# Complex linear attention and two expert layers on one core: results kept in quarters of 32 rows, block ends multiplied in three levels

## The chip, the cores and the metric

The kernel runs on one core of a Trainium2 chip. The metric is the device time of one execution in microseconds (us). PE is TensorE, DVE is VectorE, ACT is ScalarE, POOL is GpSimd, and SP is the engine on whose queue nearly all transfers are issued.

## The reference

A recurrence with complex decay per channel over 768 steps for 4 batches of 8 heads of 48 channels, then a dense layer with `h * cos(h)`, then a layer of 8 experts of which each token takes one:

```
a_n = a * min(|a|, 0.999) / (|a| + 1e-6)
S   = a_n[t] * S + k[t] v[t]^T          # complex S, 48 x 48 a head
y[t] = q[t] . real(S)
x = y as [3072, 384];  h = x @ w_in;  g = h * cos(h);  x = g @ w_out
e = argmax(x @ w_gate);  out = gate * sigmoid * (relu(x @ w1[e]) @ w2[e])
```

## The kernel before, in words

The tokens are 24 chunks of 128, six to a batch, and two chunks make a unit, so there are 12 units. A unit passes three stages:

- **The scan** (`scan`): on DVE and ACT. `normal` makes the normalised decay out of `a_t` (with a reciprocal root on ACT, `root`), `core` multiplies the decays up in blocks of 8 by 8 (seven steps along the block, then the block ends, lines 305 to 317, then the ends into the blocks, lines 320 to 331), `inverse` makes the reciprocals (a second root on ACT, line 248), and `post` multiplies q and k. Twenty small DMAs (`out_`, lines 369 to 372) bring the result to the tiles `qkr`, by head. All elementwise products of `tt` have line 205 in the profile.
- **Attention** (`attn`): for each chunk PE turns k (line 423), multiplies scores `sc` (438), DVE masks them to `pt`, and PE multiplies the results: `pt` with v (457) and, from a batch's second chunk on, the carried state `tp` with q (462). Two heads stand in one column of `pv_t`, at rows 0 and 64, 48 rows each; ACT copies `pv_t` to `x` rounded (466) and DVE takes the rest (the low part of `x`). Heads 6 and 7 stand in a fourth column, and six DMAs a chunk (488, 489) bring them into the gaps of 16 rows that the other three columns leave. Then the state is updated (473) and its halves are exchanged by DMA (481, 482).
- **The dense layer**: in eight steps s a unit, `mm1` (509, 18 products of 128x256, three each of a high and a low part) waits for `x`; `act2` (517 to 519: square, sine, square) and `act3` (548) follow; `mm2` (564, 8 records) multiplies by w_out. The `h` tiles have two buffers, which `gated` (738 to 742, which multiplies w_out by the gates' weights, through ACT copies) also takes during unit 0. `weights` decodes the weights in the first units on DVE and ACT.

ACT holds one table of functions at a time: sine needs one and the reciprocal root another, and each change is an ACT_TABLE_LOAD. Routing scatters rows by expert to DRAM, and from some 700 us on the experts' products run (`second`). A scheduler of the tile framework orders the instructions of each engine by a simulation when the program is built; `behind` adds an order without a wait. Zero rows for the scatter (493, 495) are issued on SP behind the last of the six DMAs of units 1 and 2.

Of the kernel before, what the change touches and what calls it, by code (L numbers as in the profile page):

```python
# [79 lines left out]
def host_layout(x):  # L80

    f = np.float32
    d = {}
    pq, pa = order_q(), order_a()

    def scan(p, order):
        z = p.transpose(0, 1, 3, 2).reshape(B, DM, NCB, C)[:, channels()][..., order]
        z = z.reshape(B, 3, 128, UPB, UC, C).transpose(0, 3, 2, 4, 1, 5)
        return z.reshape(NU, 128, NCOL, C)

    d["a"] = np.ascontiguousarray(np.stack([scan(x["a_re"], pa), scan(x["a_im"], pa)], 2))
    d["qk"] = np.ascontiguousarray(np.stack([scan(x["q"], pq), scan(x["k"], pq)], 2))
    v = x["v"].transpose(0, 2, 1, 3).reshape(NCH, C, DM)[:, pq]
    d["v"] = np.ascontiguousarray(v)
    rows = np.zeros((3, 128), np.int64)
    for i in range(3):
        for p in range(128):
            h, e = 2 * i + p // 64, p % 64
            if e >= 48:
                h, e = 6 + p // 64, 16 * i + e - 48  # L100
# [24 lines left out]
    d["rk"] = rk  # L125
    d["xz"] = np.zeros((256, ROW), np.int32)
    d["xz"][:, NO] = NT
    d["xz"] = d["xz"].view(f)
    tok = np.zeros((NCH, 128), np.int32)
    for c in range(NCH):  # L130
        tok[c] = (c // NCB) * S + (c % NCB) * C + pq
    d["ids"] = np.ascontiguousarray(tok.T)
    return d


def build(tc, ap, out, force=False):
# [56 lines left out]
    nb = sp.tile([128, 2, 2 * NCOL, 8], F32, name="nb")  # L193
# [5 lines left out]
    fg = sp.tile([128, 3, 2, NCOL], F32, name="fg")  # L199
    qflat = qkt.rearrange("p a b c d -> p (a b c d)")  # L200

    pv_t = ps_v.tile([128, 4, 128], F32, name="pv_t")

    def tt(e, o, a, b, op):
        return e.tensor_tensor(out=o, in0=a, in1=b, op=op)  # L205
# [26 lines left out]

    rooted = set()

    def root(u):
        rooted.add(u)
        A.activation(out=a_t[:, 2], in_=nt[:, 1], func=AF.Abs_reciprocal_sqrt)

    def inverse(u, ua):

# [5 lines left out]
        mark["add", u] = tt(V, r, sq[:, 0], sq[:, 1], ADD)  # L246
        yield
        A.activation(out=y, in_=r, func=AF.Abs_reciprocal_sqrt)
        A.activation(out=q, in_=y, func=AF.Square)
        if ua is not None:  # L250
            root(ua)
        yield
        tt(V, r, r, q, MUL)
        yield
# [36 lines left out]
    def core(u):  # L291
# [10 lines left out]
            yield  # L302
        if u + 1 < NU:
            load_a(u + 1)
        V.tensor_scalar(out=nb[:, 0], in0=lb[:, 1, :, 7], scalar1=-1.0, scalar2=None, op0=MUL)
        V.tensor_copy(nb[:, 1], lb[:, 1, :, 7])
        V.tensor_copy(pb[:, :, :, 1], lb[:, :, :, 7, 0])
# [8 lines left out]
        V.tensor_scalar(out=nb[:, 0, :, 1:8], in0=pb[:, 1, :, 1:8], scalar1=-1.0, scalar2=None, op0=MUL)  # L316
        V.tensor_copy(nb[:, 1, :, 1:8], pb[:, 1, :, 1:8])
        yield
        k = 2 * n * 56
        t1, t2 = (qflat[:, k * i:k * (i + 1)].rearrange("p (r c j b) -> p r c j b", r=2, c=n, j=8) for i in range(2))  # L320
        bc = [128, n, 8, 7]
        for r in range(2):
            tt(V, t1[:, r], lb[:, r, :, :, 1:8], pb[:, 0, :, 1:8].unsqueeze(2).to_broadcast(bc), MUL)
            yield
            tt(V, t2[:, r], lb[:, 1 - r, :, :, 1:8], nb[:, r, :, 1:8].unsqueeze(2).to_broadcast(bc), MUL)
            yield
        sq = squares(u + 1) if u + 1 < NU else iter(())
        next(sq, None)
        la = l_t.rearrange("p r c (h j b) -> p (r c h) j b", h=2, j=8)[..., 1:8]
        tt(V, la, t1.rearrange("p r c j b -> p (r c) j b"), t2.rearrange("p r c j b -> p (r c) j b"), ADD)  # L330
        yield
        gates(u)
        yield
# [71 lines left out]
    x_t = {}  # L405
    st = {}

    def attn(u):
        x = xp.tile([128, 2, 4, UC * C], F32R, name="x")
        x_t[u] = x  # L410
        kn_t = {}
        vt = {}
        for cc in range(UC):
            vt[cc] = vp.tile([128, DM], F32, name="vt")
# [16 lines left out]
        for cc in range(UC):  # L431
            c = (u % UPB) * UC + cc
            pt = {}
            for g in range(2):
# [7 lines left out]
            tp = None  # L442
            if c > 0:
                s_, ss = st["s"], st["ss"]
                tp = at1.tile([96, H, D], F32, name="tp")
# [3 lines left out]
                tt(V, tp, s_, ss, ADD)  # L449
                yield  # L450
            for g in range(2):
                t = qkr[cc, g]
                for i in range(2):
                    pr = 2 * g + i
                    for hh in range(2):
                        h = 2 * pr + hh
                        PE.matmul(pv_t[64 * hh:64 * hh + 48, pr], lhsT=vt[cc][:, h * D:(h + 1) * D],
                                  rhs=pt[g][:, 2 * i + hh], start=True, stop=c == 0)
                    if c > 0:
                        for hh in range(2):  # L460
                            h = 2 * pr + hh
                            PE.matmul(pv_t[64 * hh:64 * hh + 48, pr], lhsT=tp[:, h],
                                      rhs=t[:, 2 * i + hh, 0, 0:C], start=False, stop=True)
            yield
            xs_ = x[:, :, :, cc * C:(cc + 1) * C]
            A.copy(xs_[:, 0], pv_t)  # L466
# [2 lines left out]
            if c < NCB - 1:  # L469
                m = ps_m.tile([128, 512], F32, name="m")  # L470
                mu = m[0:96, 0:DM].rearrange("p (h d) -> p h d", h=H)
                for h in range(H):
                    PE.matmul(mu[:, h], lhsT=kn_t[cc][:, h].rearrange("p r d -> p (r d)"), rhs=vt[cc][:, h * D:(h + 1) * D],  # L473
                              start=True, stop=True)
                s_ = at1.tile([96, H, D], F32, name="s_")
                ss = at1.tile([96, H, D], F32, name="ss")
                if c == 0:
                    A.copy(s_, mu)
                else:
                    tt(V, s_, mu, tp, ADD)  # L480
# [4 lines left out]
            xb = x.bitcast(F32)  # L485
            cs = slice(cc * C, (cc + 1) * C)
            for i in range(3):
                SY.dma_start(xb[48:64, :, i, cs], xb[16 * i:16 * i + 16, :, 3, cs])
                pad = SY.dma_start(xb[112:128, :, i, cs], xb[64 + 16 * i:64 + 16 * i + 16, :, 3, cs])
            if u in (1, 2) and cc == UC - 1:  # L490
                mark["pad"] = pad
                for a0 in range(NE * CAP // 2 * (u - 1), NE * CAP // 2 * u, 256):
                    behind(SY.dma_start(xs[a0:a0 + 256], ap["xz"]), "pad")
                if u == 1:
                    behind(SY.dma_start(xs0, ap["xz"]), "pad")
            yield


# [751 lines left out]
    if True:  # L1250
# [7 lines left out]
        V.memset(pv_t, 0.0)  # L1258
        V.tensor_copy(acc, smt[:, 1, 0])
        G.tensor_copy(top, smt[:, 3])  # L1260
        V.memset(eb, 0.0)
# [114 lines left out]
```

## Time and profile before

| | |
|---|---|
| median of 3 runs | 973.82 us (973.53 to 974.1) |
| the profiled execution, its own time | 972.88 us |
| its span, first to last instruction | 971.1 us |
| PE busy | 894.8 us (92%) |
| DVE busy | 664.3 us (68%) |
| ACT busy | 582.0 us (60%) |
| ACT_TABLE_LOAD by lines 518, 237, 248 | 20, 11 and 9, of 1283 ns each |
| DMAs of `x` into the gaps | 144, 16 KB each |

A row of a timeline begins with start and duration in us; xN is the number of records merged in it, and a bracket gives the idle time before it and what ended that. A product of 32-bit floats is two records on PE, one of the rounded type is one. A busy PE is not PE at its peak, so what a stretch costs is read from starts.

### The profile page before, as it was taken

What the parts mean: (1) busy time and instruction counts of PE and PEld (TensorE: products, weight loads), DVE (VectorE), ACT (ScalarE), POOL (GpSimd) and SP (SyncE); (2) the same over time, 40 slices, a digit from 0 to 9 for tenths busy, and PEclk for the clock granted to TensorE, in tenths of its full rate; (3) what the DMA queues carried; (4) which work ended last, traced back from release to release, by engine and by line L of the source; (5) the groups of instructions that cost most, each with busy time, mean ns of one, the idle gap of its engine ahead of it and who ended that gap; (6) DMA issues with size and microseconds to landing.
All of it is one profiled execution on the core that took longest, in us unless ns stands there. A gap on an engine that the chain in (4) does not pass through costs nothing.

```text
span 971.1 us, 16175 instructions
## 1 busy us (share of the span) xinstructions
PE 894.8 (92%) x5701; PEld 756.5 (78%) x5701; DVE 664.3 (68%) x1498; ACT 582.0 (60%) x1252; POOL 134.3 (14%) x246
## 2 busy tenths in 40 slices
PE   0566897999999999999999999999999999999997
PEld 0455685877777787777777778789899899999997
DVE  6989885887779786979698788445664553355521
ACT  6684866757574848585757665365773453355521
POOL 0010001002123002020312121101121110312111
PEclk9999999999999999999999999999999999999999
DMA  9813046345333223232333231440328532554100
GB/s 328 313 43 106 20 114 207 100 120 167 102 85 122 66 95 85 90 95 90 89 101 85 97 96 47 115 142 22 106 76 259 167 128 66 175 182 140 25 28 33
DMA packets 69789, 109.93 MB, mean 113 GB/s; under 512 B 14063, under 2 KB 51327, under 8 KB 69428
## 3 DMA queue, kind: packets, MB, share of 16 engines
q1 hardware_dynamic: 62724, 98.72, 32.9%
q0 software_dynamic: 6976, 10.10, 3.1%
q8 instruction: 47, 0.77, 0.3%
q14 instruction: 42, 0.34, 0.1%
HBM read 74.20 MB, written 21.86 MB: 99 GB/s over the span
## 4 chain that ended last, share of the span: by engine, by line
PE 50%; DVE 19%; ACT 11%; DMA 8%; issue 6%; SPq 4%; POOL 0%; DVEq 0%; another core or an unknown queue 0%; ACTq 0%; POOLq 0%
PE o L564 12%; PE h L952 10%; PE h L509 10%; PE p L976 6%; PE p L968 4%; DVE t L205 3%; DVE qkt L205 2%; DMA a_t<-in_a_dram 2%; PE sc L438 2%; DVE l_t L205 1%; DVE g L548 1%; DMA xs<-in_xz_dram 1%; DVE pt L205 1%; PE m L473 1%; DVE nt L205 1%
## 5 line engine op out<-in xcount | busy, mean ns | idle before, releaser
L509 PE MATMUL h<-x,wi 128*128 128x256 f32 x1728 | 247.7, 294 | 14.9 <-DMA x<-x 5.6
L564 PE MATMUL o<-wo,g 128*128 128x400 f32 x672 | 246.2, 506 | 0.0
L509 PEld LDWEIGHTS h<-x,wi 128*128 128x128 f32 x1728 | 218.9, 191 | 34.4 <-issue 8.7
L564 PEld LDWEIGHTS o<-wo,g 128*128 128x128 f32 x672 | 121.2, 192 | 72.2 <-issue 4.4
L952 PE MATMUL h<-xe,w1t 128*128 128x384 f32 (+6 forms) x576 | 118.7, 349 | 0.0
L956 DVE SCALAR_TENSOR_TENSOR hh<-h,hh 128x384 fp32r<-128x384 f32 (+6 forms) x64 | 37.2, 582 | 117.5 <-ACT hh L955 116.9
L952 PEld LDWEIGHTS h<-xe,w1t 128*128 128x128 f32 x576 | 101.8, 188 | 5.2
L517 ACT ACTIVATE g<-h 128x512 f32<-128x512 f32 x96 | 57.1, 594 | 79.6 <-PE h L509 75.7
L955 ACT ACTIVATE hh<-h 128x384 fp32r<-128x384 f32 (+6 forms) x64 | 32.8, 514 | 114.1 <-PE h L952 107.5
L548 DVE SCALAR_TENSOR_TENSOR g<-g,h 128x512 f32<-128x512 f32 x96 | 65.5, 682 | 43.5 <-ACT g L519 42.3
L572 POOL DMA_INDIRECT xs<-rows,si x46 | 55.7, 1211 | 172.0 <-ACT x L466 41.0
L976 PE MATMUL p<-w2t,hh 128*128 128x384 f32 (+1 forms) x384 | 76.7, 343 | 0.0
L976 PEld LDWEIGHTS p<-w2t,hh 128*128 128x128 f32 (+1 forms) x384 | 66.0, 186 | 1.5 <-DVE hh L956 0.3
L519 ACT ACTIVATE g<-g 128x512 f32<-128x512 f32 x96 | 60.8, 633 | 1.8
L438 PEld LDWEIGHTS sc<-qkr 96*128 96x128 f32 x384 | 51.5, 203 | 11.7 <-issue 3.5
L438 PE MATMUL sc<-qkr 96*128 96x128 f32 x384 | 57.0, 293 | 3.8 <-DMA qkr<-qkt 2.4
L518 ACT ACTIVATE g<-h 128x512 f32<-128x512 f32 x96 | 57.6, 600 | 1.8
L205 POOL TENSOR_TENSOR fg<-l_t,m 128x12 f32<-128x12 f32 x24 | 4.7, 215 | 373.5 <-DVE l_t L205 241.8
L572 POOL DMA_INDIRECT out_dram<-o,tok x28 | 34.6, 1234 | 149.6 <-issue 57.4
L968 PE MATMUL p<-hh,w2t 128*128 128x448 f32 (+2 forms) x216 | 47.6, 359 | 0.0
L205 DVE TENSOR_TENSOR t<-l_t,a_t 128x192 f32<-128x192 f32 x144 | 45.0, 352 | 1.4
L205 DVE TENSOR_TENSOR qkt<-l_t,qk_t 128x1536 f32<-128x1536 f32 (+1 forms) x26 | 41.2, 1630 | 0.3
(299 smaller groups left out, 1501.7 us busy)
## 6 DMA issues: line engine op xcount, KB each, us to landing
stg<-in_w_dram SPq DMA_DIRECT2D x32, 768.0 KB
qkr<-qkt SPq DMA_DIRECT2D x96, 146.2 KB
a_t<-in_a_dram SPq DMA_DIRECT2D x12, 768.0 KB
qk_t<-in_qk_dram SPq DMA_DIRECT2D x12, 768.0 KB
xs<-in_xz_dram SPq DMA_DIRECT2D x17, 401.0 KB
raw<-in_w_in_dram SPq DMA_DIRECT2D x7, 768.0 KB
raw<-in_w_out_dram SPq DMA_DIRECT2D x7, 768.0 KB
vt<-in_v_dram SPq DMA_DIRECT2D x24, 192.0 KB
```

The costliest lines, as they stand in the source:

```text
L205: return e.tensor_tensor(out=o, in0=a, in1=b, op=op)
L438: PE.matmul(sc[:, h], lhsT=t[:, h, 1, 0:C], rhs=t[:, h, 0, 0:C], start=True, stop=True)
L509: PE.matmul(h[:, i], lhsT=wis[s][:, wi, kk, i * 128:(i + 1) * 128], rhs=x_t[u][:, xi, kk], start=n == 0, stop=n == 8)
L517: A.activation(out=g, in_=h, func=AF.Square, accum_out=hck[:, u * NS + s:u * NS + s + 1])
L518: mark["sin"] = A.activation(out=g, in_=h, func=AF.Sin, scale=0.5)
L519: A.activation(out=g, in_=g, func=AF.Square, scale=float(np.sqrt(2.0)))
L548: V.scalar_tensor_tensor(out=g, in0=g, scalar=1.0, in1=hps.pop((u, s)), op0=SUB, op1=MUL)
L564: PE.matmul(o, lhsT=a[:, i, cs], rhs=w[:, i], start=s == 0 and n == 0 and i == 0, stop=s == NS - 1 and n == len(prods) - 1 and i == 1)
L572: sc = G.indirect_dma_start(in_offset=None, oob_is_err=False, **kw)
L952: PE.matmul(h, lhsT=w[:, wi, kk, f * 128:(f + 1) * 128], rhs=x[:, xi, kk], start=n == 0, stop=n == 8)
L968: PE.matmul(o2[e][d][:, 0:c], lhsT=w[:, wi, f, d * 128:(d + 1) * 128], rhs=hh[:, hi], start=f == 0 and n == 0, stop=f == KE - 1 and n == 2)
L976: mm = PE.matmul(o2[e][j][0:w_, 0:DM], lhsT=hh[:, hi, j * w_:(j + 1) * w_], rhs=w[:, wi, f], start=f == 0 and n == 0, stop=f == KE - 1 and ...
```

## The change

Each head's 48 results are split in 32 and 16. The first 32 of heads 0 to 3 fill the four quarters of column 0 of `pv_t`, those of heads 4 to 7 column 1, and the last 16 of two heads share a quarter of column 2. For the shared quarter v and the state get columns of zeros beside them (`vt` and `tp` become 4 pairs of 128), so that two products add up in one quarter. A product is 32 columns wide, and there are 32 instead of 16 in a chunk with a state, 16 instead of 8 in one without. `x` uses three of its four columns, the DMAs into gaps are gone, and the rows of w_in are laid out to match. The block ends are a product over distances 1, 2 and 4 in place of six steps in a row, and the negated copies `nb` are gone: sign is in SUB and ADD, and the last sum of `core` is two instructions. The root of unit u+1 is ordered behind the square of unit u's inverse.

```
-    pv_t = ps_v.tile([128, 4, 128], F32, name="pv_t")
+    pv_t = ps_v.tile([128, 3, 128], F32, name="pv_t")
+    tp = at1.tile([96, 4, 128], F32, name="tp")
+    tps = tp[:, :, 16:112]
...
-    def root(u):
+    def root(u, *after):
         rooted.add(u)
-        A.activation(out=a_t[:, 2], in_=nt[:, 1], func=AF.Abs_reciprocal_sqrt)
+        behind(A.activation(out=a_t[:, 2], in_=nt[:, 1], func=AF.Abs_reciprocal_sqrt), *after)
...
-        A.activation(out=q, in_=y, func=AF.Square)
+        mark["rs"] = A.activation(out=q, in_=y, func=AF.Square)
         if ua is not None:
-            root(ua)
+            root(ua, "rs")
...
-        for i in range(2, 8):
-            t1, t2 = t12[:, 0, :, 0:n], t12[:, 1, :, 0:n]
-            tt(V, t1, pb[:, :, :, i - 1], lb[:, 0:1, :, 7, i - 1].to_broadcast([128, 2, n]), MUL)
-            tt(V, t2, pb[:, ::-1, :, i - 1], nb[:, :, :, i - 1], MUL)
-            yield
-            tt(V, pb[:, :, :, i], t1, t2, ADD)
-            yield
+        for d, a, b in ((1, last[..., 1:7], last[..., 0:6]), (2, pb[..., 3:8], pb[..., 1:6]), (4, pb[..., 5:8], pb[..., 1:4])):
+            t1, t2 = (t12[:, i].rearrange("p r (c b) -> p r c b", b=8)[..., 0:7 - d] for i in range(2))
+            bc = [128, 2, n, 7 - d]
+            tt(V, t1, a, b[:, 0:1].to_broadcast(bc), MUL)
+            tt(V, t2, a, b[:, 1:2].to_broadcast(bc), MUL)
+            yield
+            tt(V, pb[:, 0, :, d + 1:8], t1[:, 0], t2[:, 1], SUB)
+            tt(V, pb[:, 1, :, d + 1:8], t1[:, 1], t2[:, 0], ADD)
+            yield
...
+            srcs = [(vt[cc], [pt[h // 4][:, h % 4] for h in range(H)])]
+            if c > 0:
+                srcs.append((tp, [qkr[cc, h // 4][:, h % 4, 0, 0:C] for h in range(H)]))
+            for kk in range(2):
+                for n, (a, r) in enumerate(srcs):
+                    for g in range(4):
+                        h = 4 * kk + g
+                        w = 32 + 32 * (h % 2)
+                        PE.matmul(pv_t[32 * g:32 * g + 32, kk], lhsT=a[:, h // 2, w:w + 32], rhs=r[h],
+                                  start=n == 0, stop=n == len(srcs) - 1)
+            for n, (a, r) in enumerate(srcs):
+                for odd in range(2):
+                    for g in range(4):
+                        PE.matmul(pv_t[32 * g:32 * g + 32, 2], lhsT=a[:, g, 96 * odd:96 * odd + 32], rhs=r[2 * g + odd],
+                                  start=n == 0 and odd == 0, stop=n == len(srcs) - 1 and odd == 1)
...
-            for i in range(3):
-                SY.dma_start(xb[48:64, :, i, cs], xb[16 * i:16 * i + 16, :, 3, cs])
-                pad = SY.dma_start(xb[112:128, :, i, cs], xb[64 + 16 * i:64 + 16 * i + 16, :, 3, cs])
```

The scheduler makes another order out of it. The rows below name lines of each kernel's own file; up to 3 lines lie between them. Three places follow.

ACT, unit 0, behind the second copy of `pv_t` to `x`. In the kernel before (466 is the copy; 227 and 228 square the decays of unit 2; 517 to 519 are `act2`):

```order
L466 CAST x<-pv_t 128x4x128
L227 ACTIVATE a_t<-a_t 128x768
L228 ACTIVATE nt<-a_t 128x768
L517 ACTIVATE g,hck<-h 128x512
L518 ACT_TABLE_LOAD
L518 ACTIVATE g<-h 128x512
L519 ACTIVATE g<-g 128x512
L517 ACTIVATE g,hck<-h 128x512
```

In the changed kernel (469 is the copy, 230 and 231 the squares, 514 to 516 `act2`):

```order
L469 CAST x<-pv_t 128x3x128
L514 ACTIVATE g,hck<-h 128x512
L515 ACT_TABLE_LOAD
L515 ACTIVATE g<-h 128x512
L516 ACTIVATE g<-g 128x512
L514 ACTIVATE g,hck<-h 128x512
L230 ACTIVATE a_t<-a_t 128x768
L231 ACTIVATE nt<-a_t 128x768
```

The first step's `act2` and the start of the second's now stand ahead of the squares.

PE, where unit 0's products meet unit 1's first scores. In the kernel before (423 turns k, 738 and 741 are `gated`, 438 the scores, 473 the state, 509 `mm1`):

```order
L423 MATMUL m<-ident,qkt 128x128 x3
L741 MATMUL h<-wg,raw 128x16 x3
L738 MATMUL h<-ident,raw 128x128 x3
L438 MATMUL sc<-qkr 128x128 x6
L473 MATMUL m<-vt,kn 96x48 x6
```

In the changed kernel (426 turns k, 735 and 738 are `gated`, 506 `mm1`, 476 the state, 441 the scores):

```order
L426 MATMUL m<-ident,qkt 128x128 x3
L735 MATMUL h<-ident,raw 128x128 x3
L506 MATMUL h<-x,wi 128x256 x18
L476 MATMUL m<-vt,kn 96x48 x8
L738 MATMUL h<-wg,raw 128x16 x3
L441 MATMUL sc<-qkr 128x128 x2
```

A whole step of `mm1` and one chunk's state now stand ahead of the scores.

ACT, the last two `gated` copies of unit 0 (742 with `rawr`; 244 to 249 are unit 2's `inverse`). In the kernel before:

```order
L742 COPY rawr<-h 128x16
L726 COPY wo<-rawr 128x16
L739 COPY rawr<-h 128x384
L244 ACTIVATE qkt<-l_t 128x1536
L517 ACTIVATE g,hck<-h 128x512
L518 ACT_TABLE_LOAD
L518 ACTIVATE g<-h 128x512
L248 ACT_TABLE_LOAD
L248 ACTIVATE qkt<-nt 128x768
L519 ACTIVATE g<-g 128x512
L742 COPY rawr<-h 128x16
```

In the changed kernel (739 with `rawr` is the same copy; 230 and 231 square the decays of unit 3):

```order
L739 COPY rawr<-h 128x16
L723 COPY wo<-rawr 128x16
L230 ACTIVATE a_t<-a_t 128x768
L231 ACTIVATE nt<-a_t 128x768
L736 COPY rawr<-h 128x384
L514 ACTIVATE g,hck<-h 128x512
L739 COPY rawr<-h 128x16
```

No table load stands between the two copies any more; the squares, which stood ahead of both before, stand between them.

## Rows read from the trace of the kernel before

**Rows 1.** The page's first line.
```profile
span 971.1 us, 16175 instructions
```

**Rows 2.** Busy time by stretch: length, then each engine's busy us, clock, DMA share.
```profile
0.00:180.00 180.00, 119.05 (x680) 97.64 (x681) 146.35 (x291) 122.81 (x267) 9.02 (x43) 0.97 0.46 155
180.00:610.00 430.00, 420.99 (x2854) 329.06 (x2854) 348.82 (x813) 282.97 (x600) 71.24 (x148) 1.00 0.33 97
610.00:971.00 361.00, 354.78 (x2169) 329.76 (x2167) 169.14 (x395) 176.20 (x386) 54.04 (x55) 1.00 0.35 112
```

**Rows 3.** Timeline of PE at the first unit's `mm1`.
```profile
93.22 0.77 PE L509 MATMUL h<-x,wi 128*128 128x256 f32 x2 [4.66 <-DMA x<-x]
104.68 0.51 PE L509 MATMUL h<-x,wi 128*128 128x256 f32 x2 [3.38 <-DVE g L548]
```

**Rows 4.** Timeline of ACT in the same stretch.
```profile
88.61 0.59 ACT L466 CAST x<-pv_t 128x512 fp32r<-128x512 f32 x1 [4.60 <-PE pv_t L462]
99.18 0.85 ACT L227 ACTIVATE a_t<-a_t 128x768 f32<-128x768 f32 x1 [9.99 <-DMA a_t<-in_a_dram]
```

**Rows 5.** Timeline of PE where units 0 and 1 meet.
```profile
132.66 1.68 PE L438 MATMUL sc<-qkr 96*128 96x128 f32 x12 [0.21 <-DMA qkr<-qkt]
...
151.00 2.39 PE L509 MATMUL h<-x,wi 128*128 128x256 f32 x18
...
156.20 0.63 PE L738 MATMUL h<-ident,rawr 128*128 128x128 f32 x3 [2.20 <-ACT raw L742]
156.87 4.65 PE L564 MATMUL o<-wo,g 128*128 128x400 f32 x8
...
170.25 2.03 PE L509 MATMUL h<-x,wi 128*128 128x256 f32 x10 [3.47 <-ACT rawr L742]
```

**Rows 6.** Timeline of ACT where units 0 and 1 meet.
```profile
121.85 0.24 ACT L358 COPY qkt<-fg 128x24 f32<-128x24 f32 x1
...
155.98 0.16 ACT L742 COPY raw<-h 128x16 f32<-128x16 f32 x1
...
167.48 1.28 ACT L248 ACT_TABLE_LOAD   x1
...
170.04 0.15 ACT L742 COPY rawr<-h 128x16 f32<-128x16 f32 x1
```

**Rows 7.** Timeline of DVE: first instruction of a block end, first behind it.
```profile
94.32 0.21 DVE L305 TENSOR_SCALAR nb<-l_t 128x96 f32<-128x96 f32 x1
...
98.53 0.85 DVE L205 TENSOR_TENSOR qkt<-l_t,pb 128x672 f32<-128x672 f32 x1
```

**Rows 8.** Groups of DVE by form: busy us, mean ns of one, idle before.
```profile
L205 DVE TENSOR_TENSOR t<-l_t,a_t 128x192 f32<-128x192 f32 x144 | 45.0, 352 | 1.4
...
L205 DVE TENSOR_TENSOR x<-pv_t,x 128x512 fp32r<-128x512 f32 x24 | 16.4, 682 | 1.5 <-ACT x L466 1.5
L205 DVE TENSOR_TENSOR pb<-t 128x24 f32<-128x24 f32 x72 | 14.6, 202 | 1.9
```

**Rows 9.** Timeline of PE, a lone run of scores and a run of results.
```profile
435.26 1.73 PE L438 MATMUL sc<-qkr 96*128 96x128 f32 x14
436.74 2.25 PE L509 MATMUL h<-x,wi 128*128 128x256 f32 x17
...
440.93 0.42 PE L457 MATMUL pv_t<-pt,vt 128*48 128x128 f32 x4
...
442.83 0.94 PE L564 MATMUL o<-wo,g 128*128 128x400 f32 x2
```

**Rows 10.** Timeline of PE, a run of results cut in two pieces.
```profile
146.95 0.43 PE L457 MATMUL pv_t<-pt,vt 128*48 128x128 f32 x4
147.31 0.94 PE L564 MATMUL o<-wo,g 128*128 128x400 f32 x2
```

**Rows 11.** Who waited for whom: us in total, times, longest.
```profile
DVE s__5808 L205 <- DMA x<-x: 5.4, 1, 5.4
```

**Rows 12.** Groups of ACT: busy us, mean ns of one, idle before.
```profile
L518 ACT ACT_TABLE_LOAD x20 | 25.7, 1283 | 0.3
```

More of the change, by code (lines that the diff above doesn't have):

```diff
@@ L92, in host_layout @@
     d["qk"] = np.ascontiguousarray(np.stack([scan(x["q"], pq), scan(x["k"], pq)], 2))
-    v = x["v"].transpose(0, 2, 1, 3).reshape(NCH, C, DM)[:, pq]
-    d["v"] = np.ascontiguousarray(v)
+    v = x["v"].transpose(0, 2, 1, 3).reshape(NCH, C, 4, 2, D)[:, pq]
+    d["v"] = np.zeros((NCH, C, 4, 128), f)
+    d["v"][..., 16:32], d["v"][..., 32:64] = v[..., 0, 32:], v[..., 0, :32]
+    d["v"][..., 64:112] = v[..., 1, :]
     rows = np.zeros((3, 128), np.int64)
@@ L97, in host_layout @@
         for p in range(128):
-            h, e = 2 * i + p // 64, p % 64
-            if e >= 48:
-                h, e = 6 + p // 64, 16 * i + e - 48
+            h, e = 4 * i + p // 32, p % 32
+            if i == 2:
+                h, e = 2 * (p // 32) + (e < 16), 32 + e % 16
             rows[i, p] = h * D + e
@@ L192, in build @@
     t12 = sp.tile([128, 2, 2, NCOL * 16], F32, name="t12")
-    nb = sp.tile([128, 2, 2 * NCOL, 8], F32, name="nb")
     pb = sp.tile([128, 2, 2 * NCOL, 8], F32, name="pb")
@@ L304, in core @@
             load_a(u + 1)
-        V.tensor_scalar(out=nb[:, 0], in0=lb[:, 1, :, 7], scalar1=-1.0, scalar2=None, op0=MUL)
-        V.tensor_copy(nb[:, 1], lb[:, 1, :, 7])
-        V.tensor_copy(pb[:, :, :, 1], lb[:, :, :, 7, 0])
-        yield
-        for i in range(2, 8):
-            t1, t2 = t12[:, 0, :, 0:n], t12[:, 1, :, 0:n]
-            tt(V, t1, pb[:, :, :, i - 1], lb[:, 0:1, :, 7, i - 1].to_broadcast([128, 2, n]), MUL)
-            tt(V, t2, pb[:, ::-1, :, i - 1], nb[:, :, :, i - 1], MUL)
+        last = lb[:, :, :, 7]
+        V.tensor_copy(pb[:, :, :, 1], last[..., 0])
+        for d, a, b in ((1, last[..., 1:7], last[..., 0:6]), (2, pb[..., 3:8], pb[..., 1:6]), (4, pb[..., 5:8], pb[..., 1:4])):
[3 more added lines that the diff above has]
+            tt(V, t2, a, b[:, 1:2].to_broadcast(bc), MUL)
             yield
-            tt(V, pb[:, :, :, i], t1, t2, ADD)
+            tt(V, pb[:, 0, :, d + 1:8], t1[:, 0], t2[:, 1], SUB)
+            tt(V, pb[:, 1, :, d + 1:8], t1[:, 1], t2[:, 0], ADD)
             yield
-        V.tensor_scalar(out=nb[:, 0, :, 1:8], in0=pb[:, 1, :, 1:8], scalar1=-1.0, scalar2=None, op0=MUL)
-        V.tensor_copy(nb[:, 1, :, 1:8], pb[:, 1, :, 1:8])
-        yield
         k = 2 * n * 56
@@ L324, in core @@
             yield
-            tt(V, t2[:, r], lb[:, 1 - r, :, :, 1:8], nb[:, r, :, 1:8].unsqueeze(2).to_broadcast(bc), MUL)
+            tt(V, t2[:, r], lb[:, 1 - r, :, :, 1:8], pb[:, 1, :, 1:8].unsqueeze(2).to_broadcast(bc), MUL)
             yield
@@ L328, in core @@
         next(sq, None)
-        la = l_t.rearrange("p r c (h j b) -> p (r c h) j b", h=2, j=8)[..., 1:8]
-        tt(V, la, t1.rearrange("p r c j b -> p (r c) j b"), t2.rearrange("p r c j b -> p (r c) j b"), ADD)
+        for r, op in ((0, SUB), (1, ADD)):
+            tt(V, lb[:, r, :, :, 1:8], t1[:, r], t2[:, r], op)
         yield
@@ L406, in build, with pairs @@
     st = {}
+    def pairs(t):
+        return t.rearrange("d (p i) e -> d p (i e)", i=2)
     def attn(u):
-        x = xp.tile([128, 2, 4, UC * C], F32R, name="x")
+        x = xp.tile([128, 2, 4, UC * C], F32R, name="x")[:, :, 0:3]
         x_t[u] = x
@@ L413, in attn @@
         for cc in range(UC):
-            vt[cc] = vp.tile([128, DM], F32, name="vt")
+            vt[cc] = vp.tile([128, 4, 128], F32, name="vt")
             SY.dma_start(vt[cc], ap["v"][u * UC + cc])
@@ L441, in attn @@
                 yield
-            tp = None
             if c > 0:
                 s_, ss = st["s"], st["ss"]
-                tp = at1.tile([96, H, D], F32, name="tp")
                 t, bc = qkc[cc], [96, H, D]
@@ L448, in attn @@
                 tt(V, ss, ss, t[:, :, 0, C + 1:C + 2].to_broadcast(bc), MUL)
-                tt(V, tp, s_, ss, ADD)
+                tt(V, tps, pairs(s_), pairs(ss), ADD)
                 yield
[L451 to L463, printed above, removed]
+            srcs = [(vt[cc], [pt[h // 4][:, h % 4] for h in range(H)])]
[13 more added lines that the diff above has]
+                                  start=n == 0 and odd == 0, stop=n == len(srcs) - 1 and odd == 1)
             yield
@@ L472, in attn @@
                 for h in range(H):
-                    PE.matmul(mu[:, h], lhsT=kn_t[cc][:, h].rearrange("p r d -> p (r d)"), rhs=vt[cc][:, h * D:(h + 1) * D],
+                    PE.matmul(mu[:, h], lhsT=kn_t[cc][:, h].rearrange("p r d -> p (r d)"), rhs=vt[cc][:, h // 2, 16 + 48 * (h % 2):64 + 48 * (h % 2)],
                               start=True, stop=True)
@@ L479, in attn @@
                 else:
-                    tt(V, s_, mu, tp, ADD)
+                    tt(V, pairs(s_), pairs(mu), tps, ADD)
                 SY.dma_start(ss[0:48], s_[48:96])
@@ L484, in attn @@
                 yield
-            xb = x.bitcast(F32)
-            cs = slice(cc * C, (cc + 1) * C)
-            for i in range(3):
-                SY.dma_start(xb[48:64, :, i, cs], xb[16 * i:16 * i + 16, :, 3, cs])
-                pad = SY.dma_start(xb[112:128, :, i, cs], xb[64 + 16 * i:64 + 16 * i + 16, :, 3, cs])
             if u in (1, 2) and cc == UC - 1:
-                mark["pad"] = pad
                 for a0 in range(NE * CAP // 2 * (u - 1), NE * CAP // 2 * u, 256):
-                    behind(SY.dma_start(xs[a0:a0 + 256], ap["xz"]), "pad")
+                    behind(SY.dma_start(xs[a0:a0 + 256], ap["xz"]), ("x", u))
                 if u == 1:
-                    behind(SY.dma_start(xs0, ap["xz"]), "pad")
+                    behind(SY.dma_start(xs0, ap["xz"]), ("x", u))
             yield
@@ L1257, in build @@
         SY.dma_start(wg, ap["wg"].rearrange("(k p) l -> p k l", p=128))
-        V.memset(pv_t, 0.0)
+        V.memset(tp, 0.0)
         V.tensor_copy(acc, smt[:, 1, 0])
```

## The prediction

> **What bounds the kernel now.** I read the stretches first, then PE's gaps, then the engine behind each gap. The stretches [rows 2] show three regimes. From 180 us to the end PE is busy 776 of 791 us: there only PE's own work and its last 15 us of gaps count, and whatever DVE, ACT or SP save is hidden. In the first 180 us PE is busy 119, and DVE with 146 and ACT with 123 carry the start. So the change is worth two things: what it does to PE's work at any time, and what it takes out of PE's 61 us of gaps in the start. Of these, the first products of the start cannot come sooner than the scan of unit 0, so I look behind it: 4.66 us before the first `mm1` and 3.38 before its third step [rows 3], 2.20 and 3.47 where unit 0 ends [rows 5].
>
> **PE's results.** A run of 4 records takes 0.36 us (146.95 to 147.31) [rows 10], one of 32 takes 1.90 (440.93 to 442.83) [rows 9]: 0.055 a record, and 0.14 for each time that PE turns to such products. Scores, which use all columns and stream the same 128, take 1.48 for 14 records, 0.106 each [rows 9]. So today's two heads, one in either half of the columns, pass side by side. The change doubles the records (704 to 1408, two a product) and puts them on quarters. If four pass side by side, a record costs 0.0265 and a chunk the same as now; if only two can, 0.055 as now, and a chunk with a state costs 32 more records, 1.76 us. Less than now is excluded, since there are only four quarters and the stream is as long. I take four: the two halves already load and stream apart from each other, and nothing in these rows ties them to being two. The end that I keep is 20 chunks x 1.76 + 4 x 0.88 = 38.7 us. The Trainium skill (TensorEngine Tiling (Array Packing), Available Configurations) counts 128x32 as four independent tiles; no run here shows that yet. By the order of instructions the results stand in 44 runs instead of 37: 7 x 0.14 = **1.0 us slower**.
>
> **The first dense step.** The wait of 4.66 us is for the DMAs into gaps, which go. `mm1` then needs only ACT's copy, which ends at 89.20 (88.61 + 0.59) [rows 4], so it starts some 4.0 us earlier. What is late next is `act2`: ACT sat idle 9.99 us for the decays of unit 2 until 99.18 [rows 4], and only behind their squares came the square and sine that PE waited for at 104.68. In the new order `act2` of the first step stands ahead of the squares, in that idle time. So at the third step PE is up to 7 us ahead. Most of it is given back: unit 1's scores start at 132.66, on DMAs of `qkr` [rows 5], which carry the gates that ACT copies at 121.85 [rows 6]. ACT has more ahead of that copy in the new order, two more table loads among it (five instead of three from the first sine to the last sine of `inverse` of unit 1), 2.6 us by 1283 ns each [rows 12]; so I leave the scores where they are. What stays is the work that PE does before instead of after them: a step of `mm1`, 2.39 us [rows 5]. I take **2.4 us**, between 0 and 5.
>
> **Where unit 0 ends.** PE waits 2.20 us for the copy at 155.98, and 3.47 for the one at 170.04, whose buffer the next `mm1` needs [rows 5, 6]. The first stood behind ACT's wait for decays; the second behind two table loads, of which one is the row at 167.48. In the new order no load stands between the two copies and the first is ahead of the squares. A third loss is inside the 8 records at 156.87, which take 4.65 us [rows 5], while 2 of their kind go at 442.83 in 0.94 [rows 9]. Both gaps are 5.7 us; the second copy now stands behind the squares and may wait with them, so I take **4.7 us**, between 0 and 7.5.
>
> **Block ends.** In unit 1 they took 94.32 to 98.53, 4.21 us with nothing between [rows 7]: 23 instructions of about 202 ns, each level waiting for the one before. The three levels are 12 instructions and a copy. Between 202 ns for 24 columns and 352 for 192 [rows 8] a column costs 0.9 ns, so products of 144, 120 and 72 columns take 309, 288 and 245 ns, and sums of 72, 60 and 36 take 245, 234 and 213; twice their sum and the copy is 3.25 us end to end. That is 1.0 us less at least. The last sum in two instructions gives back one fixed part, some 0.2. The low part of `x` has 384 columns instead of 512, 0.13 us less [rows 8]. Over 12 units DVE sheds some 13 us, and ACT 14 table loads, 18 us; behind 180 us both lie beside a full PE and cost or bring nothing. On the path is unit 0 alone, where other work fills the steps' waits: **0.7 us**, between 0 and 1.2.
>
> **The rest.** The 144 issues leave SP, v's transfers grow by a third, and the zero rows follow the low part of `x` directly. One DVE wait of 5.4 us for the DMAs into gaps [rows 11] goes, and PE's late gaps are 9.0 us in 180 to 610 [rows 2]: I take **1.0 us**, between 4 gained and 3 lost, since the new order makes waits of its own. If the cover of 180 to 610 failed, it would be ACT or the scan that decided, and that is a rival below.
>
> **Sum.** 2.4 + 4.7 + 0.7 + 1.0 - 1.0 = 7.8 us. The profiled execution took 972.88 us (its span is 971.1 [rows 1], so 1.8 lie around it), and the median of the runs is 0.94 above it. 972.88 - 7.8 = 965.1 in its terms, **966.0** beside the median of 973.82.
>
> **Rivals.** (1) *The quarters don't pass four at a time.* The place is each chunk's results, 1408 records; the price at the other end is 38.7 us, so 966.0 + 38.7 = 1004.7. It decides from 32 ns a record on, where 1408 records of 5.5 ns more use up the 7.8 us. For it: PE must take eight loads and products in the 0.106 us in which it now takes four, and no row shows that rate. Against it: the halves show side-by-side passage. I give this rival 0.12. The Trainium skill (TensorE: Matmul & The Clock Gate, Wait — 56ns, not 53.3ns?) has a rule that leads there: in one setting the sequencer spends about 62 ns on each product. The 55 ns a record over 32 records speaks against that rule here, though such a run is half as long as the new ones. By it a chunk of 64 records would take an estimated 4.0 us, and the kernel would come out at about 1016; 0.03 of this rival's chance is for that.
>
> (2) *Unit 2's scan is late next.* PE reaches the end of unit 0 some 7 us sooner and then waits as long for unit 2's `qkr`, whose chain over DVE, ACT and SP is as long as now. Then only 0.7 stays, less 1.0 for the runs: 973.2 in the profile's terms, 974.1, no change. Against it: the new order puts two more dense steps of unit 1 ahead of unit 2's turning of k, and a step's `mm1` alone is 2.39 us [rows 5]; and ACT has fewer loads there. 0.09.
>
> (3) *New waits behind 180 us.* The order there is another everywhere. If its gaps were twice the 9.0 us [rows 2], this would cost 9.0 beyond the forecast: 966.0 + 9.0 = 975.0. 0.05. That the roots don't share a round trip is hardly open: the orders hold 40 and 26 loads for the three lines; in unit 1 they do the opposite, and that is in the sum.
>
> **The numbers.** The forecast has 0.74. A measurement tells 0.2%, 1.9 us, from no change, so faster means below 971.9. Nearly all of the forecast's case lies there, rival 2 mostly within, rival 1 wholly above, rival 3 above or within: 0.73 faster, 0.09 same, 0.18 slower. All gains at their upper bounds, 5 + 7.5 + 1.2 + 4 - 1 = 16.7, give 957.1; the case in which the gains don't come, with only the added runs, is 974.8. So the range is 957 to 975; outside lie rival 1, half of rival 3 and the forecast's tails, some 0.19.
>
> **What would show it.** Right: starts of results 0.11 us apart for four records of different quarters, so a run of 64 near 1.9 us; first `mm1` near 89 us; no wait of PE for the last `gated` copies; gaps of PE behind 180 us that sum to no more than the 15 us of now; block ends near 3 us. Wrong: a run of 64 records near 3.6 us, or PE's gaps of the start back at unit 2's turning of k or scores.

## The result, and the profile after

The changed kernel takes **958.38 us** (957.8 to 959.71, 4 runs) beside 973.67 for the kernel before on the same chip: a ratio of 0.9842, interval 0.9824 to 0.9861, 15.3 us less. That is faster and inside the range, near its lower end, but twice the forecast's 7.8 us. The profiled execution took 959.71 us and was the slowest of the four, so the two profiled spans differ by 13.2 us and not by 15.3. Its page begins, with engine totals (compare [rows 1]):

```profile
span 957.9 us, 17275 instructions
...
PE 892.1 (93%) x6405; PEld 755.7 (79%) x6405; DVE 651.3 (68%) x1390; ACT 564.0 (59%) x1238; POOL 129.2 (13%) x246
```

The stretches, columns as in [rows 2] (length, busy us of PE, PEld, DVE, ACT, POOL, clock, DMA share, GB/s):

```profile
0.00:180.00 180.00, 127.17 (x874) 105.80 (x875) 149.14 (x274) 131.73 (x291) 7.49 (x43) 0.95 0.47 157
180.00:610.00 430.00, 422.98 (x3400) 329.80 (x3399) 338.09 (x734) 259.68 (x570) 71.91 (x153) 0.99 0.35 100
610.00:957.00 347.00, 341.94 (x2134) 320.08 (x2132) 164.05 (x383) 172.62 (x379) 49.80 (x50) 1.00 0.34 109
```

PE's idle time in the first 180 us fell from 61 to 53 us, and in 180 to 610 from 9.0 to 7.0. The timeline of PE through the start, changed kernel; these rows answer to [rows 3, 5]:

```profile
89.60 6.52 PE L506 MATMUL h<-x,wi 128*128 128x256 f32 x36 [0.60 <-ACT x L469]
98.43 2.39 PE L506 MATMUL h<-x,wi 128*128 128x256 f32 x18 [2.31 <-DVE g L545]
...
132.95 0.69 PE L441 MATMUL sc<-qkr 96*128 96x128 f32 x4
...
145.02 2.38 PE L506 MATMUL h<-x,wi 128*128 128x256 f32 x18
...
150.32 2.93 PE L561 MATMUL o<-wo,g 128*128 128x400 f32 x8
...
157.99 2.39 PE L506 MATMUL h<-x,wi 128*128 128x256 f32 x18 [0.32 <-ACT rawr L739]
```

A place that both kernels reach tells how far ahead the changed one is. The first `mm1` is 3.6 us ahead, its third step 6.3; unit 1's scores start where they did (132.95 beside 132.66); unit 0's last step is 6.0 ahead (151.00, now 145.02), and unit 1's second step **12.3** (170.25, now 157.99). The waits of 2.20 and 3.47 are one of 0.32. Then some is lost. The same product at unit 3's first step, before and after:

```profile
267.19 2.37 PE L509 MATMUL h<-x,wi 128*128 128x256 f32 x18
```

```profile
260.57 2.37 PE L506 MATMUL h<-x,wi 128*128 128x256 f32 x18
```

That is a lead of **6.6**, and at the end of the span it is **13.2** (971.1 - 957.9). So the change gains 12.3 at the start, gives 5.7 back in unit 2, and gains 6.6 behind it. Most of that last part is gaps of PE that close. From this step of `mm1` to one that both kernels reach at 634.24 and 622.10, before and after:

```profile
267.19:634.24 367.05, 359.36 (x2433) 280.51 (x2431) 287.68 (x664) 237.81 (x504) 63.96 (x124) 1.00 0.32 90
```

```profile
260.57:622.10 361.53, 359.70 (x2848) 280.47 (x2847) 280.04 (x601) 220.91 (x491) 59.72 (x124) 1.00 0.32 90
```

The changed kernel is 5.5 us quicker there (367.05, 361.53) with the same busy time of PE: it idles 1.8 us where PE idled 7.7.

What is given back is one wait, in PE's timeline and then in ACT's:

```profile
210.50 2.85 PE L561 MATMUL o<-wo,g 128*128 128x400 f32 x8
217.25 4.21 PE L506 MATMUL h<-x,wi 128*128 128x256 f32 x18 [3.91 <-DVE g L545]
```

```profile
207.65 1.49 ACT L247 ACTIVATE qkt<-l_t 128x1536 f32<-128x1536 f32 x1 [4.09 <-DMA xs<-in_xz_dram]
209.16 1.28 ACT L251 ACT_TABLE_LOAD   x1
...
212.07 0.83 ACT L240 ACTIVATE a_t<-nt 128x768 f32<-128x768 f32 x1
212.81 0.58 ACT L514 ACTIVATE g<-h 128x512 f32<-128x512 f32 x1
...
213.49 1.28 ACT L515 ACT_TABLE_LOAD   x1
```

ACT serves the scan (square, load, two roots) ahead of `act2`, with a second load between `act2`'s square and sine; `act3` and PE wait for it, at unit 2's third step of `mm1`. The 18 records behind the wait then take 4.21 us instead of 2.39, so the 3.91 cost 5.7 in all.

The results do pass four abreast. Timeline of PE, a lone run of 64 records (it answers to [rows 9]):

```profile
329.46 0.43 PE L460 MATMUL pv_t<-pt,vt 128*32 128x128 f32 x8
...
330.36 0.62 PE L465 MATMUL pv_t<-pt,vt 128*32 128x128 f32 x16
330.80 0.62 PE L465 MATMUL pv_t<-qkr,tp 96*32 96x128 f32 x16
331.35 0.86 PE L506 MATMUL h<-x,wi 128*128 128x256 f32 x5
```

From 329.46 to 331.35 is 1.89 us: less 0.14 for the turn, 0.027 a record. And a block end, DVE's timeline (compare [rows 7]):

```profile
93.66 0.19 DVE L309 COPY pb<-l_t 128x24 f32<-128x24 f32 x1
...
96.05 0.30 DVE L208 TENSOR_TENSOR pb<-t 128x36 f32<-128x36 f32 x2
97.69 0.69 DVE L545 SCALAR_TENSOR_TENSOR g<-g,h 128x512 f32<-128x512 f32 x1 [1.33 <-ACT g L516]
98.29 3.16 DVE L208 TENSOR_TENSOR qkt<-l_t,pb 128x672 f32<-128x672 f32 x4
```

It takes 2.69 us (93.66 to 96.35) instead of 4.21, but DVE then stands 1.33 for an `act3`, and the products behind start at 98.29 where they started at 98.53.

### The profile page after: what moved, and what is told of

It reads as the page before. It is cut to its first block, busy times and chain, and to the rows that moved or that the text cites. A ratio compares the mean times of both kernels' runs of the same rounds, so it can differ in the third digit from the quotient of the medians.

```text
span 957.9 us, 17275 instructions
## 1 busy us (share of the span) xinstructions
PE 892.1 (93%) x6405; PEld 755.7 (79%) x6405; DVE 651.3 (68%) x1390; ACT 564.0 (59%) x1238; POOL 129.2 (13%) x246
## 4 chain that ended last, share of the span: by engine, by line
PE 69%; ACT 10%; DVE 9%; issue 4%; DMA 4%; SPq 2%; another core or an unknown queue 1%; POOL 1%; POOLq 0%; DVEq 0%; ACTq 0%
PE o L561 19%; PE h L506 17%; PE h L949 10%; PE p L973 6%; PE p L965 4%; PE sc L441 3%; PE pv_t L460 2%; PE m L476 2%; PE pv_t L465 2%; DVE qkt L208 1%; ACT g L514 1%; DMA a_t<-in_a_dram 1%; ACT g L515 1%; PE tp L836 1%; ACT raw L701 1%
## 5 line engine op out<-in xcount | busy, mean ns | idle before, releaser
L569 POOL DMA_INDIRECT xs<-rows,si x46 | 52.1, 1133 | 210.1 <-DVE l_t L208 43.3
L441 PE MATMUL sc<-qkr 96*128 96x128 f32 x384 | 54.7, 287 | 0.0
```

The lines of the kernel that those rows point to most:

```text
L441: PE.matmul(sc[:, h], lhsT=t[:, h, 1, 0:C], rhs=t[:, h, 0, 0:C], start=True, stop=True)
L569: sc = G.indirect_dma_start(in_offset=None, oob_is_err=False, **kw)
```

## The experiments

Each run is given with its median and its ratio to the kernel before on the same chip. "Hunks" are those of the diff above.

### Each part alone, as the scheduler orders it

The first question was which of the three parts carries the gain. The kernel before with the quarters' hunks alone, with the root's alone, with the block ends' alone, and the changed kernel without the root's:

```
quarters:   +pv_t = ps_v.tile([128, 3, 128], F32, name="pv_t")   +PE.matmul(pv_t[32 * g:32 * g + 32, kk], ...
            -SY.dma_start(xb[48:64, :, i, cs], ...   (all six a chunk)
roots:      -            root(ua)
            +            root(ua, "rs")
block ends: -        for i in range(2, 8):
            +        for d, a, b in ((1, last[..., 1:7], last[..., 0:6]), ...
```

> The kernel before with the quarters alone: no copies into gaps, wide tiles of v and state, 32 products a chunk; block ends and roots as before (50 table loads). Theory A, the copies into gaps carry the gain: nearly all of the 15.3 us, 958 to 963 us, with the gaps of 4.66, 2.20 and 3.47 us of the start gone. Rival B, the table loads carry the part that is regained behind unit 2 (some 6 us): 964 to 968. Rival C, the order that the scheduler happens to find decides: the three parts apart don't add up to 15.3, by more than 4 us.

Measured: 976.48, ratio 1.0045 (1.003 to 1.006): **slower**.

> The kernel before with the one order of the roots alone (34 table loads instead of 46). Theory A: the loads lie beside a full PE, 972 to 974 us, no change. Rival B: 966 to 970, gained in units 3 to 7 (lead at equal milestones of PE grows there from 0 to some 6 us). Rival C: anything within 5 us of 973.7, with the lead made at one place where the order differs.

Measured: 970.05, ratio 0.9974 (0.9959 to 0.999).

> The kernel before with the block ends in three levels alone. Theories A and B: only unit 0's block end is on the path, 0 to 1.2 us, 972.5 to 973.7; no gap of PE at the start goes. Rival C: off by more than 2 us to either side.

Measured: 979.16, ratio 1.0065 (1.0046 to 1.0084): slower.

> The changed kernel without the order of the roots: quarters and block ends (50 table loads). Theory A: 958 to 961 us, like the changed kernel within 2 us. Rival B: 963 to 966. Rival C: no bound, but then the lead over the kernel before differs already at unit 2.

Measured: 969.28, ratio 0.9967 (0.9952 to 0.9983).

Theories A and B both fall, and C holds. By ratios the three parts alone add up to 8 us lost, where together they gain 15; taking the roots' hunk out of the change costs 12, while put in alone it brings 2.5. In the run with quarters alone PE idles 14.7 us in 180 to 610 (before: 9.0), in this stretch of its trace:

```profile
180.00:610.00 430.00, 415.31 (x3287) 320.47 (x3286) 347.94 (x811) 282.16 (x592) 64.31 (x148) 1.00 0.33 97
```

Each edit gives the scheduler another program, and it finds another order everywhere. So these runs measure an order as much as a part.

### Work and order apart

The next kernels hold every engine to a given order: behind the build, each instruction is put behind its predecessor in that order, with no wait added. Where the numbers of instructions differ, the block end's and the results' are laid into the places of their counterparts.

```
+def pin(nc, tc):
...
+        seq = [own[k] for k in np.frombuffer(zlib.decompress(base64.b85decode(blob)), "<u2")]
+        for a, b in zip(seq, seq[1:]):
+            tc.add_manual_dep(b, a.name, mybir.DependencyInfo(mybir.DependencyClass.NoSync, mybir.DependencyReason.DATA),
+                              reason="issue order")
```

> The changed kernel's instructions, every engine held to the order of the kernel before (50 loads fewer or more follow from that order alone: the roots stand where they stood). Theory W, the parts save by themselves: 963 to 967 us, near the forecast. Theory O, the gain lies in the order that the change lets the scheduler find: 970 to 974, with act2 of the first step behind the squares and two waits of 2 to 3.5 us for the last gated copies as before, whatever the quarters bring at the first mm1.

Measured: **959.85**, ratio 0.9867 (0.9838 to 0.9897).

> The kernel before, with its copies into gaps, half-column results and six-step block ends, every engine held to the order of the changed kernel (the 144 copies alone stand free). Theory W: 972 to 975 us, and the first mm1 again near 93 us. Theory O: 960 to 965, with the first mm1 near 93 us too, but without the two waits for the last gated copies, and with 32 table loads.

Measured: **1001.85**, ratio 1.0305 (1.0276 to 1.0333).

> Quarters and no copies into gaps, block ends in six steps, held to the order of the changed kernel. Theory W: 965 to 968 us (all but the block ends). Theory O: 958 to 961, 1 to 3 us above the changed kernel, since unit 1's block end stands on the path as well as unit 0's. Alone in its own order it took 976.5.

Measured: 961.5, ratio 0.9883 (0.9854 to 0.9912).

> Block ends in three levels, copies into gaps and half-column results as before, held to the order of the changed kernel. Theory W: 971 to 974 us. Theory O: 958 to 963, 0 to 5 us above the changed kernel for the copies into gaps at the start. Alone in its own order it took 979.2.

Measured: 999.05, ratio 1.0266 (1.0239 to 1.0294).

Theory O falls as it stood: the new order without the work is 29 us slower, and the old order with the work gives 13 of the 15.3 us. The work carries the gain, and does so better than theory W had it (963 to 967 us); the new order adds 2 to 5 by the two measurements of the changed kernel (0.9842 here, 0.9817 below), and the intervals overlap or touch. But order alone decides whether the work's gain is seen: the same quarters take 976.5, 961.5 and (below) 965.3 in three orders. What makes the scheduler's own order for the quarters so much worse was not followed up and stays open. (In the two runs with copies in the new order the copies stood free, so an unlucky place of theirs may be part of the 29: in the first of them PE waits 6.8 us in 180 to 610 for their landing, and 11.8 for the state `tp`.)

The old order with all the work also shows where the gain sits when nothing moves. Its PE timeline at the places of [rows 3, 5]:

```profile
87.61 1.44 PE L506 MATMUL h<-x,wi 128*128 128x256 f32 x5 [0.58 <-ACT x L469]
...
102.94 3.36 PE L506 MATMUL h<-x,wi 128*128 128x256 f32 x14 [7.91 <-DVE g L545]
```

```profile
154.04 2.95 PE L561 MATMUL o<-wo,g 128*128 128x400 f32 x8
...
165.93 4.42 PE L506 MATMUL h<-x,wi 128*128 128x256 f32 x19 [3.47 <-ACT rawr L739]
```

The first `mm1` is 5.6 us ahead, but a wait of 7.91 eats most of that, as `act2` again stands behind the squares; at unit 1's second step 4.3 remain (170.25, 165.93). All the rest up to 13.3 (971.1 - 957.8) comes behind it, a little in each unit.

### Which work, and by what

In the same old order: the quarters alone, the block ends alone, and all the work with the 144 copies put back, once landing on what `mm1` reads and once beside it, in the fourth column of `x` that nothing reads.

```
put back: +                SY.dma_start(xb[48:64, :, i, cs], xb[48:64, :, i, cs])
          +                pad = SY.dma_start(xb[112:128, :, i, cs], xb[112:128, :, i, cs])
aside:    +                SY.dma_start(xb[16 * i:16 * i + 16, :, 3, cs], xb[48:64, :, i, cs])
          +                pad = SY.dma_start(xb[64 + 16 * i:80 + 16 * i, :, 3, cs], xb[112:128, :, i, cs])
```

> Quarters and no copies into gaps, block ends in six steps, every engine held to the order of the kernel before. All the work in this order took 959.9 us. Theory P, the copies into gaps are what cost (their landing at the start, SP's queue and the engines' turn behind 180 us): 960 to 963 us, with PE's waits behind 180 us at 2 to 4 us instead of 9. Theory Q, the shorter block ends bring the scan forward in every unit and so end PE's late waits: 966 to 970, with late waits of 6 us or more.

Measured: 965.35, ratio 0.9914 (0.9885 to 0.9944); its profiled span is 960.3.

> Block ends in three levels alone, every engine held to the order of the kernel before. Theory P: 970 to 973 us, 0 to 3 below the kernel before (the forecast had 0.7 for unit 0 alone). Theory Q: 962 to 967, with PE's late waits halved. In the order that the scheduler finds for it, it took 979.2.

Measured: 973.42, ratio 0.9999 (0.9981 to 1.0016).

> All the work of the change (roots as before) in the order of the kernel before, with the 144 copies put back in number, size and place in SP's queue; each carries rows of x onto themselves, so that nothing is computed otherwise. Theory P: 969 to 973 us, first mm1 back near 93 us and late waits of PE back at 7 to 10 us. Theory Q: 960 to 963, but for the start (at most 4 us).

Measured: **975.73**, ratio 1.0026 (1.0006 to 1.0045).

> As the run with the 144 copies put back, in the same order and with the same number and size, but each copy goes into the unused fourth column of x, so that no product waits for its landing: what stays is its place in SP's queue. Theory L, PE's waits for the landing are the cost: 958 to 962 us, as without copies. Theory S, the copies' turn on SP (each waits there for the low part of x, with the transfers of qkr behind it) is the cost: 968 to 973, late waits of PE at 7 to 10 us; only the start (first mm1 near 88 us) is as without copies, some 0 to 4 us below the run with the copies put back (975.7).

Measured: **970.87**, ratio 0.9985 (0.9969 to 1.0002).

Theory P holds and Q falls, though the quarters alone and the copies put back come out 2 to 3 us above the ranges that P gave them. In this order the copies are the cause: with them back, the whole gain is gone, though quarters and short block ends stay. And most of it is not their landing. The run with the copies aside differs from the one without copies in nothing but the copies, that is in their place on SP and their traffic, and loses 1.18% or 11.5 us; landing on `mm1`'s operand costs another 0.4%, 4 us (the two intervals just miss each other). The time and the late waits are as theory S had them; its start is not, since the first `mm1` comes at 89.70 and not near 88. PE's stretch of 180 to 610, all the work without copies:

```profile
180.00:610.00 430.00, 428.08 (x3457) 337.19 (x3457) 341.34 (x743) 281.47 (x594) 74.38 (x153) 1.00 0.34 100
```

and with the copies aside:

```profile
180.00:610.00 430.00, 422.15 (x3356) 330.11 (x3355) 338.53 (x734) 280.43 (x598) 68.16 (x148) 1.00 0.34 100
```

PE idles 1.9 us without copies and 7.9 with them (before: 9.0), and passes 101 records more in that stretch. So of the 11.5 us about 6 are gaps of this stretch; another 3.7 are gaps of the first 180 us (PE idles 59.5 there without copies, 63.2 with them). What SP does in that time, by its queue's waits (line, waited for: us in all, times, longest), in the kernel before:

```profile
SPq L369 <- DVE qkt L205: 62.3, 7, 13.5
SPq L488 <- DVE x L205: 38.2, 5, 19.7
...
SPq L488 <- DVE pt L205: 12.8, 3, 6.5
```

and with the copies aside (492 is the copy):

```profile
SPq L492 <- DVE x L208: 33.9, 5, 18.9
...
SPq L492 <- DVE pt L208: 12.9, 3, 5.5
```

For over 50 us of the 430 SP stands in front of a copy that waits for DVE, up to 19.7 at once, and issues nothing that is queued behind it: the pieces of `qkr`, the halves of the state, the next loads. But a stand costs only if something behind it is ready, and the run without copies stands no less: there the row of line 369 is 83.9 us. What is held up shows where a transfer's data are ready. One exchange of the state just behind that stretch, with the copies aside, by the view of its tile, and what SP did just before by its timeline:

```profile
L208 DVE TENSOR_TENSOR s__6013<-m,tp x1: 554/554/554, 615.4 to 615.4; 96x384 f32<-96x384 f32 x1
L485 SPq DMA_DIRECT2D ss<-s__6013 x1: 567/567/567, 619.2 to 619.2; - x1
```

```profile
617.13 0.71 SPq L492 DMA_DIRECT2D x<-x  x1
...
618.52 0.59 SPq L492 DMA_DIRECT2D x<-x  x1
```

The same exchange without copies:

```profile
L208 DVE TENSOR_TENSOR s__5887<-m,tp x1: 554/554/554, 603.8 to 603.8; 96x384 f32<-96x384 f32 x1
L484 SPq DMA_DIRECT2D ss<-s__5887 x1: 531/531/531, 604.4 to 604.4; - x1
```

The state is ready at 616.0 (615.4 and 0.55) and its exchange is issued 3.2 us later, behind three copies that wait for nothing; without copies it is issued at once. Over the 14 or 15 exchanges that become ready in 180 to 610 these delays sum to 6.9 us with the copies aside, 7.7 in the kernel before and 0.8 without copies. (The changed kernel, without copies but in its own order, has 6.6, so what such a delay costs depends on the order too.) Six copies in a row take SP 3.84 us from start to start (566.75 to 570.59), so all 144 take it an estimated 92 us. So the issue of a copy holds up what is queued behind, and not only a copy's wait; how the 11.5 us divide between the two was not measured.

PE's own waits in that stretch of the kernel before are the sum of many small ones:

```profile
PE sc L438 <- DMA qkr<-qkt: 2.2, 2, 1.4
PE pv_t L462 <- DVE tp L205: 1.6, 2, 1.3
PE h L509 <- DVE g L548: 1.3, 2, 0.7
```

In all the work without copies the first of these is 0.2 and the other two are not there. That a given wait of PE goes back to a given delay on SP is argued, not shown. The copies aside also move their bytes, 16 KB each; against this as the cause stands that the share of the DMA engines is 0.34 in both stretches above. The Trainium skill (DMA: Bandwidth & Descriptors, Issuing engines are not separate DMA queues) says that starting transfers from several engines saves only the time of initiating them, which is usually small beside the transfer. Here that time is 0.64 us of SP a copy, and it counts, since what is queued behind the copies has to wait for it.

The block ends alone bring nothing in the old order; beside the quarters (0.9867 against 0.9914, 4.6 us, or 2.5 by the two profiled spans) they may bring something, but the intervals overlap.

### The give-back at unit 2, and two orders meant to lie below both

Up to unit 7 the changed kernel's order leads, behind it the old order gains more. A kernel with all the work takes the one up to unit 7's first `mm1` and the other from there; a second one moves `act2` and `act3` ahead of the two roots at 209 us:

```
 ACT, spliced order       ACT, act2 first
 L247 square of l_t       L247 square of l_t
 L251 load, root          L514, L515, L516 act2
 L252 square              L251 load, root
 L240 root                L252 square
 L514 act2's square       L240 root
 L515 load, sine          L514 next act2's square
```

> All the work of the change, held to the order of the changed kernel up to unit 7's first mm1 and to the order of the kernel before from there. At that place the changed kernel led the kernel before by 13.5 us and the work in the old order by 8.7; behind it the old order gained 4.6 more. If the two orders' leads add, which the theory that the order decides says: 953 to 956 us, below both. If the later gain in the old order only makes good what it lost earlier (a lead that PE can't use): 957 to 960, like the changed kernel.

Measured: 956.0, ratio 0.9816 (0.9788 to 0.9845).

> The spliced order with one thing moved: at 209 us ACT does act2 of unit 2's first step (square, sine, square) ahead of the two roots of unit 3's inverse, and DVE its act3 ahead of the product that waits for them; the table loads are as many as before. If ACT's order made PE's wait of 3.92 us there: that wait goes, and with it what PE loses at the half clock behind it (3.4 us recorded at 0.5), 3 to 6 us less than the spliced order, 950 to 953 us. If unit 3's scan is late next (its turned k stands on PE some 10 us further on, and its chain is now 1.9 us later): the wait comes back at unit 3's turning of k, 955 to 958.

Measured: 953.8, ratio 0.9798 (0.9781 to 0.9816).

> The changed kernel, every engine held to its own order: a control for what holding an order costs, and the time beside which the two runs above stand. 957 to 960 us by every theory.

Measured: 954.95, ratio 0.9817 (0.9796 to 0.9838). That is below its own range: on this chip the changed kernel is 17 us below the kernel before. So neither of the two can be told from it; the two orders' leads add by less than the 4.6 us that the first expectation had, and holding an order costs nothing that is seen.

In the second kernel the wait of 3.92 us for `act3` does go, but another takes its place. PE and then ACT:

```profile
218.23 3.03 PE L561 MATMUL o<-wo,g 128*128 128x400 f32 x4 [3.37 <-ACT rows L585]
```

```profile
215.89 1.28 ACT L515 ACT_TABLE_LOAD   x1
...
217.68 0.50 ACT L585 ACTIVATE rows<-o 128x400 f32<-128x400 f32 x1
```

PE now waits for unit 1's output copies, which stand on ACT behind the same roots and the load of the sine. At unit 2's seventh `mm1` both kernels are at the same time, 249.3 and 249.4 by their traces. So it looks as if the place were ACT's, with what it has to do there for unit 3's scan, and not a matter of which of its consumers stands last; only this one other order was tried. Neither expectation had this wait, and 953.8 lies between their two ranges.

## Why the prediction was half right

**What bounds the kernel.** The reading of the start holds. The step that **failed** is the sentence that behind 180 us "whatever DVE, ACT or SP save is hidden": for SP it isn't, and this is the main error. PE's gaps of 9.0 us in 180 to 610 were read as a remainder. In one and the same order they are 1.9 without copies and 7.9 with the copies aside, and the copies aside cost 11.5 us in all, about 6 of them in these gaps; in the changed kernel's own order the gaps behind unit 2 fall from 7.7 to 1.8. The rows that the prediction rests on are PE's, DVE's and ACT's; none is of SP's queue.

**PE's results.** Right: a record costs 0.027 us where 0.0265 was taken, a run of 64 takes 1.9. Rival 1 falls, and with it the rule of 62 ns a product: by that a run of 64 would last 4.0 us. The same section of the Trainium skill (TensorE: Matmul & The Clock Gate, Wait — 56ns, not 53.3ns?) has starts never closer than some 25 ns, however short the product; the 27 here lie just above that. What the seven added runs cost was not measured alone.

**The first dense step.** The mechanism is right: first `mm1` at 89.60 (near 89), third step 6.3 ahead (up to 7), scores of unit 1 where they were. What stays was mis-sized. At unit 0's last step the lead is 6.0 and not 2.4, but the two kernels have not done the same work by then: the results of unit 1's second chunk, 1.9 us, now stand behind that step, and one product of `gated`, 0.7 us, ahead of it. At equal work the lead is an estimated 4.8, inside the bounds of 0 to 5. Ahead of the scores now stand not only a step of `mm1` but also chunk products of the state and of `gated`; the forecast's own piece of order shows the eight `m<-vt,kn` and three `h<-wg,raw` there, and the sum left them out.

**Where unit 0 ends.** Right in kind, mis-sized: the lead goes to 12.3, so 7.5 instead of 4.7 at equal work, at the upper bound. Both waits go (5.67, 0.32 comes), and the "third loss" of the 8 records at 156.87, which was seen and given no price, goes too: 4.65 us then, 2.93 now. It was the clock, see below.

**Block ends.** Sized about right (2.69 us; at most 3.25 foreseen), and the path was judged right: alone in the old order they bring 0.0, with 0 to 1.2 forecast.

**The rest.** This is the term that fails most, by the step named first: it has the 144 issues that leave SP, but at no price of their own. It was put at 1.0 us, "between 4 gained and 3 lost", and measured 6.6 from unit 3's first step to the end, and 9.0 (from 4.3 to 13.3) behind the start in the old order.

**What was not in the sum.** The give-back of 5.7 us at unit 2. Rival 2 had the kind (the scan late next, once PE is ahead) at 0.09, but one unit early, with `qkr` as what is waited for and with the whole gain lost. Here it is unit 3's `inverse` on ACT, and it takes less than half of the lead. Rival 3 had new waits behind 180 us at 0.05. This is one, but PE's gaps there fall in sum from 15.3 us to 13.0, where rival 3 had the 9.0 of 180 to 610 double.

So 2.4 + 4.7 stand for 12.3, the give-back stands for nothing, and 1.0 and 0.7, less 1.0, for 6.6: 12.3 - 5.7 + 6.6 = 13.2 against 7.8. That the sign came out as forecast owed something to luck: the quarters alone, in the order that the scheduler finds for them, are slower than before.

## What to carry to other kernels

A transfer costs the transfers behind it in its queue the time of its issue, and that of its wait if its producer is slow: before calling such an issue hidden, read how long the issuing engine is held by it, and how late what is ready behind it is issued. Where a scheduler lays the order, a part of a change is priced with the order held, since the part alone in its own order may have the other sign. A wait of PE is priced with the slow products behind it, and one that is moved away on a busy in-order engine comes back at that engine's next consumer.

## What the chip showed beside that

The gaps cost more than their length. Granted clock, as a share of 2.4 GHz, in two stretches of the kernel before, around the wait of 2.20 us that ends at 156.20 [rows 5], and in two of the changed one (columns as above):

```profile
153.00:157.00 4.00, 1.76 (x14) 1.47 (x13) 3.93 (x10) 3.07 (x8) 0.00 (x0) 1.00 0.25 75
157.00:160.60 3.60, 3.60 (x6) 1.85 (x7) 2.79 (x3) 3.57 (x6) 0.00 (x0) 0.53 1.01 304
```

```profile
213.30:217.20 3.90, 0.04 (x1) 0.00 (x0) 2.69 (x6) 3.87 (x11) 3.21 (x5) 0.92 0.14 53
216.60:223.40 6.80, 6.15 (x22) 5.16 (x23) 6.34 (x7) 5.28 (x13) 2.11 (x2) 0.50 0.37 104
```

After PE had been idle for 2.20 or 3.91 us of a stretch, the clock is recorded at half, 1.2 GHz, while PE is busy again: 8 records of `mm2` in 4.65 us instead of 2.93, a step of `mm1` in 4.21 instead of 2.39. So each of these two waits cost some 1.7 to 1.8 us on top. Half clock follows shorter waits too. In the changed kernel PE waits 1.29 us twice (until 122.62 and 125.50), and the step of `mm1` behind them, the one that now stands ahead of unit 1's scores, runs at half clock:

```profile
126.69 4.19 PE L506 MATMUL h<-x,wi 128*128 128x256 f32 x18
```

```profile
126.70:131.00 4.30, 4.30 (x23) 4.30 (x22) 2.99 (x3) 2.29 (x10) 0.00 (x0) 0.50 0.56 129
```
